# An eighth P buffer, seven output rows on GpSimd and a new table of order in an attention and routed-MLP kernel

## The chip, the cores and the metric

The kernel runs on one core of one Trainium2 chip. The core has TensorE (PE: matrix products into PSUM), ScalarE (ACT: activation functions), VectorE (DVE), GpSimd (POOL) and a queue engine for DMAs (SP). The metric is device microseconds of one execution. Times of several runs are given as their median; an execution taken with the hardware profiler has its own time.

## What is computed

One layer over 2048 tokens of width 448: layer norm, attention with 16 heads of 28 that share one key and one value head, a residual, and then a second layer norm whose rows feed a router; the eight tokens with the highest router score go through a gated MLP, and its weighted result is added to their rows.

```python
x = A_x                                             # [1, 2048, 448]
xn = layernorm(x)
q = xn @ wq                                         # 16 heads of 28
k, v = xn @ wk, xn @ wv                             # one head for all
p = softmax(q k^T * 28 ** -0.5)
h = x + concat_heads(p v) @ wo
n = layernorm(h)
r = n @ w_r
idx = argsort(-r)[:8]
y = (silu(n[idx] @ w_gate) * (n[idx] @ w_up)) @ w_down
out = h + n + scatter(idx, y * sigmoid(r[idx]))
```

## The kernel before

**Blocks and tiles.** The queries are cut into 4 blocks of 512 (qb) and the heads into 4 groups of 4 (g); b = 4 qb + g counts the 16 blocks. The keys are cut into 16 tiles j of 128. One (b, j) is a tile of work. Its scores are two pairs of matmuls (p = 0, 1), each pair 128 keys by 2 heads by 512 queries, which fills two PSUM banks of 512 f32 columns.

**Two ways through the softmax.** A tile goes to ScalarE or to VectorE.

- ScalarE (`act_unit`, L1008): each score pair is one exponential over 128 x 1024 (L1012), from PSUM into a slot of P, a ring of NPB = 6 slots (L309). A pair and the next one use banks 0 and 1 or 2 and 3 in turn, so a score pair must wait until the exponential before the last one is done. `act_pv` (L1015) then multiplies the two slots of a tile by the values: one group of four matmuls side by side (32 x 512 each).
- VectorE (`dve_unit`, L1020): the exponential is made out of the bits of a 16-bit number. Each score pair, in banks 4 and 5, is clamped into 16-bit integers Y (L1024), and three copies shifted by a constant (`shift`, L1028, operation on L1031) are made of the tile; four groups of value matmuls (`dve_pv`, L1036), one per copy with values scaled to fit, average the error out. Y is a ring of 3 tiles. For the tiles that `shared` marks, the third shift is done by GpSimd.

**Around the blocks.** `chunk` (L670) prepares 512 tokens at a time: statistics, normalized rows, transposes, keys and values. `q_project` makes the queries of a block two blocks ahead. `post_block` copies a block's sums (L751), sends the denominators through memory to spread them over the partitions, and scales the result on GpSimd into On (L767). When four groups are done, `out_proj` (L780) makes 128 rows of h: projection on TensorE, residual and statistics on VectorE, the inverse root on GpSimd (L795), and for qb below 2 the output row h + n (L802), a scaling of 128 x 448 f32 on VectorE into outf, which lies over x in SBUF. `out_rows` stores two such rows in one DMA of the SP queue. `first_top`, `first_max` and `second_top` search the highest router scores of the first 1536 tokens inside block 15; the small cast into topb is L856. Behind the last exponential comes a serial tail: the last block's rows, the search, the MLP for eight tokens, and an indirect store from `fin`, which lies in wq_sb.

**What sets the order.** Every operation is recorded with an engine, an assumed duration, what it reads and writes and a priority (`G.op`). `plan` (L113) goes through them as a list scheduler would and fixes the order of the instructions on each engine; the program is emitted in that order, with semaphores where needed. An engine runs its list strictly in order, so what is written behind a waiting instruction waits too. Two rules matter here. For TensorE, score pairs for ScalarE are marked `crit`: another operation is put ahead of one that will soon be ready only if it would make it late by no more than SLACK, and TensorE is left idle for it if that is shorter than WAIT. Operations marked `lock` (all of GpSimd, and VectorE's shifts and some others) are planned so that they don't overlap; a GpSimd operation gets a wait for the last such VectorE operation planned ahead of it, while VectorE gets none for GpSimd.

The priorities come from tables at the top of the file. For each block from 2 on, TILES says which key tiles go to VectorE, how many of them have the third shift on GpSimd, and an offset in time. EARLY lists the VectorE tiles of blocks 0 and 1, QUERY, ROWS and CHUNK place the projections, the output rows and the preparation. Before, the tables hold 58 + 4 = 62 tiles for VectorE, 33 of them shared, and 194 for ScalarE.

Of the kernel before, what the change touches and what calls it, by code (L numbers as in the profile page):

```python
# [16 lines left out]
SLACK, WAIT = 248.0, 240.0  # L17
# [4 lines left out]
    2: ((0, 5, 8, 13), 4, -0.95),  # L22
    3: ((0, 3, 6, 10, 13), 3, 0.94),
    4: ((2, 8, 10, 12), 2, 1.48),
    5: ((1, 4, 6, 11), 0, 1.34),
    6: ((2, 6, 11, 13), 2, -0.37),
    7: ((1, 3, 8, 11, 13), 2, 1.13),
    8: ((4, 9, 11, 13), 0, 1.08),
    9: ((5, 7, 12), 3, 0.03),
    10: ((0, 5, 8, 10, 12), 3, 1.5),  # L30
    11: ((2, 4, 9, 12), 1, -0.68),
    12: ((0, 2, 4, 8), 4, 0.5),
    13: ((0, 2, 6, 9, 11), 5, 0.63),
    14: ((2, 10, 12), 3, 1.18),
    15: ((0, 4, 8, 10), 1, 0.33),
# [3 lines left out]
EARLY = [(0, 5, 18.21), (0, 15, 22.04), (0, 4, 23.54), (1, 12, 28.01)]  # L39
QUERY = {2: 12.3, 3: 12.3, 4: 6.9, 5: 7.0, 6: 11.5, 7: 11.1, 8: 8.7, 9: 10.4, 10: 6.7, 11: 9.5, 12: 10.1, 13: 7.6}  # L40
ROWS = {
    (0, 0): 10.9, (0, 1): 7.3, (0, 2): 10.3, (0, 3): 9.3, (1, 0): 10.7, (1, 1): 11.9, (1, 2): 13.1,
    (1, 3): 9.9, (2, 0): 6.2, (2, 1): 11.4, (2, 2): 8.4, (2, 3): 9.2
}
CHUNK = (0.0, 5.1, 10.9, 36.9)
# [255 lines left out]
def _main(nc, G, sb, ps, psb, flag, scr, xs, ptab, A_x, A_wq, A_wk, A_wv, A_wo, B_w_r, B_w_gate, B_w_up, B_w_down, out,  # L301
# [8 lines left out]
    NPB = 6  # L310
# [12 lines left out]
    idi = sb("idi", [128, 128], I32)  # L323
# [45 lines left out]
    junk = sb("junk", [128, D], BF16)  # L369
    outf = x_sb[:, :, 0:D]  # L370
# [42 lines left out]
    onesb = sb("onesb", [128, 128], BF16)  # L413
    bz = sb("bz", [128, 3, 8], BF16)
    onesh = sb("onesh", [128, 128], F16)
# [4 lines left out]
    eg = sb("eg", [128, NFC, 8], F32)  # L420
    sg = sb("sg", [128, NFC, 8], F32)
# [10 lines left out]
    def pk(b):  # L432
        return ("ps", b)
# [28 lines left out]
    for i in range(4, NT, 4):  # L462
        dma(x_sb[:, i:i + 4, 0:D], x_v[:, i:i + 4, :], [("x", t) for t in range(i, i + 4)], lat=3500.0 + 400 * i,
            reads=[("x", 3)])
    G.op(PO, lambda e: e.iota(idi[:, :], [[1, 128]], base=0, channel_multiplier=-1), 250, writes=["idi"])
    G.op(PO, lambda e: e.tensor_single_scalar(ident[:, :], idi[:, :], 0, ALU.is_equal), 560,
         reads=["idi"], writes=["ident"])
# [40 lines left out]
    def kk(j, p):  # L508
        return ("K0", min(j, 2), p) if j < 4 else ("K", j // 4, p)
# [25 lines left out]
    def late_consts(gate):  # L535
# [16 lines left out]
        G.op(PO, lambda e: e.memset(onesb[:, :], 1.0), 200, writes=["onesb"])  # L552
        G.op(PO, lambda e: e.memset(bz[:, :, :], 0.0), 100, writes=["bz"])
        G.op(PO, lambda e: e.memset(onesh[:, :], 1.0), 200, writes=["onesh"])
# [6 lines left out]
        G.op(PO, lambda e: e.iota(idi[0:8, 0:96], [[1, 96]], base=0, channel_multiplier=0), 250, writes=["idi"])  # L561
# [485 lines left out]
    for m, (b, j, t) in enumerate(dve_tiles):  # L1047
        for p in range(2):
            at(t + 1.5 * p, dve_unit, m, b, j, p, t + 1.5 * p)
        for v in (1, 2, 3):  # L1050
            at(t + 1.6 + 0.5 * v, shift, m, v, b)
# [295 lines left out]
```

## Time and profile before

| | us |
|---|---|
| median of 3 runs (387.9 to 390.82) | 388.7 |
| the profiled execution, its own time | 387.67 |
| its span, first to last instruction | 385.9 |
| busy: ScalarE / TensorE / VectorE / GpSimd | 374.1 / 344.0 / 338.2 / 115.0 |
| first exponential starts | 9.47 |
| ScalarE goes on to the first instruction behind the last exponential | 365.88 |

How to read the rows that follow. A row of a timeline has the start and the length in us from the span's start, the engine, the line of the kernel, the operation, what it writes and reads (buffer numbers left out), shapes, and how many instructions the row merges. A row of a group has the shape, the count, then busy us and the mean ns of one, then the idle time of the engine just before them and what ended it. A row of windows has a stretch and its length, then for each engine the busy time and the number of instructions, then the granted clock, the share of the DMA engines and GB/s. Matmuls overlap and their ends are modelled; starts are what to go by. The granted TensorE clock is 0.984 of full speed over the span.

### The profile page before, as it was taken

To read this page: it belongs to the slowest core of one execution; us is meant where nothing else is said; L and a number is where in the kernel's file an instruction comes from. 1 tells how busy PE (TensorE), PEld (TensorE's weight loads), DVE (VectorE), ACT (ScalarE), POOL (GpSimd) and SP (SyncE) were. 2 spreads that over 40 slices of the span, in tenths; PEclk is the share of its full clock that TensorE was granted. 3 is DMA by queue.
4 is the path that set the end of the run, shared out by engine and by line. 5 is a ranking of instruction groups with operands and counts; after the bars stand their busy time and mean duration, and the time that the engine had idled before them with its cause. 6 is when DMAs were issued, how large, how long until landed. Compare 5 with 4: busy or idle time off the path is not lost.

```text
span 385.9 us, 8129 instructions
## 1 busy us (share of the span) xinstructions
PE 344.0 (89%) x3361; PEld 105.6 (27%) x3361; DVE 338.2 (88%) x613; ACT 374.1 (97%) x433; POOL 115.0 (30%) x149
## 2 busy tenths in 40 slices
PE   7799898989988999899998988999898999888945
PEld 7333222222222222222222222222222222222324
DVE  6985888888998999989999989999999998999382
ACT  6999999999999999999999999999999999999992
POOL 7440002544123112404101244402145454431100
PEclk9999999999999999999999999999999999999985
DMA  8696000100000000201001000011001010100011
GB/s 208 163 235 190 2 2 12 49 2 29 2 27 5 4 29 26 77 1 54 2 14 63 7 27 27 28 50 31 26 30 51 3 53 27 52 26 20 14 51 55
DMA packets 18045, 17.12 MB, mean 44 GB/s; under 512 B 6660, under 2 KB 15124, under 8 KB 18004
## 3 DMA queue, kind: packets, MB, share of 16 engines
q1 hardware_dynamic: 17652, 16.32, 14.7%
q8 instruction: 27, 0.44, 0.5%
q10 hardware_dynamic: 288, 0.23, 0.2%
q14 instruction: 14, 0.11, 0.1%
q0 software_dynamic: 64, 0.02, 0.0%
HBM read 11.70 MB, written 4.86 MB: 43 GB/s over the span
## 4 chain that ended last, share of the span: by engine, by line
ACT 92%; PE 3%; DVE 3%; DMA 1%; issue 0%; SPq 0%; POOL 0%; POOLq 0%
ACT P L1012 90%; PE ps L436 3%; DMA wq_sb<-in_A_wq_dram 1%; ACT xn L964 1%; DVE Y L1024 1%; DVE topb L856 0%; DVE bn L934 0%; SPq L449 0%; ACT x_sb L825 0%; DVE Y L1031 0%; ACT xnT L618 0%; POOL out_dram L1239 0%; ACT Rb L741 0%; ACT Rb L739 0%; ACT wq_pad L491 0%
## 5 line engine op out<-in xcount | busy, mean ns | idle before, releaser
L1012 ACT ACTIVATE P<-ps 128x1024 bf16<-128x1024 f32 x388 | 356.3, 1132 | 1.4 <-PE ps L436 1.3
L436 PE MATMUL ps<-Q,K 64*128 64x512 bf16 x1024 | 179.9, 385 | 29.3 <-ACT P L1012 25.0
L1024 DVE TENSOR_SCALAR Y<-ps 128x1024 int16<-128x1024 f32 x124 | 151.2, 1219 | 19.8 <-PE ps L436 19.5
L1031 DVE TENSOR_SCALAR Y<-Y 128x2048 int16<-128x2048 int16 x153 | 100.4, 685 | 0.5
L436 PEld LDWEIGHTS ps<-Q,K 64*128 64x128 bf16 x1024 | 44.7, 93 | 175.4 <-ACT P L1012 152.7
L1031 POOL TENSOR_SCALAR Y<-Y 128x2048 int16<-128x2048 int16 x33 | 62.6, 1898 | 96.4 <-DVE Y L1031 87.6
L436 PE MATMUL ps<-Y,Vs 128*32 128x512 bf16 x992 | 84.9, 383 | 0.0
L436 PE MATMUL ps<-P,Vs 128*32 128x512 bf16 x776 | 76.3, 388 | 0.1
L767 POOL TENSOR_TENSOR On<-Ot,Rb 128x512 bf16<-128x512 f32 x15 | 19.1, 1273 | 45.5 <-DVE Y L1031 30.6
L436 PEld LDWEIGHTS ps<-Y,Vs 128*32 128x32 bf16 x992 | 23.8, 95 | 27.3 <-issue 17.5
L436 PEld LDWEIGHTS ps<-P,Vs 128*32 128x32 bf16 x776 | 19.6, 93 | 42.5 <-issue 41.7
L763 POOL TENSOR_TENSOR Ls<-Ls,Lc 128x16 f32<-128x16 f32 x15 | 4.2, 280 | 68.2 <-DVE Y L1031 60.9
L436 PE MATMUL ps<-xnT,wq_pad 112*128 112x512 bf16 (+1 forms) x68 | 19.2, 371 | 0.6 <-DVE K L643 0.5
L436 PE MATMUL ps<-wo_pad,On 128*128 128x448 bf16 (+1 forms) x64 | 17.5, 358 | 1.0 <-DVE On L745 1.0
L517 DVE TENSOR_SCALAR Q<-ps,qone 128x512 bf16<-128x512 f32 x15 | 11.0, 734 | 1.7 <-PE ps L436 1.7
L795 POOL TENSOR_TENSOR hbuf<-st,nhalf 128x1 f32<-128x1 f32 x12 | 6.6, 552 | 14.3 <-DVE Y L1031 10.3
L751 DVE COPY Ot<-ps 128x512 f32<-128x512 f32 x15 | 10.3, 684 | 0.7 <-PE ps L436 0.4
L804 DVE SCALAR_TENSOR_TENSOR junk<-hbuf,w_rb 128x448 bf16<-128x448 f32 x12 | 8.1, 677 | 0.0
L789 DVE TENSOR_TENSOR hbuf<-ps,x_sb 128x448 f32<-128x448 f32 x12 | 7.4, 618 | 0.3 <-PE ps L436 0.2
L791 DVE BATCH_NORM_STATS2 bn<-hbuf 128x6 f32<-128x448 f32 x12 | 7.4, 618 | 0.1
L719 DVE TENSOR_SCALAR K<-ps,ksc,kb 128x512 bf16<-128x512 f32 x6 | 4.6, 803 | 3.3 <-PE ps L436 3.3
L1239 POOL DMA_INDIRECT out_dram<-wq_sb,idxc x1 | 0.9, 930 | 20.8 <-DVE wq_sb L1238 20.8
(209 smaller groups left out, 172.1 us busy)
## 6 DMA issues: line engine op xcount, KB each, us to landing
Rb<-h_scr SPq DMA_DIRECT2D x15, 256.0 KB
h_scr<-hbuf SPq DMA_DIRECT2D x12, 225.0 KB, 2.2
out_dram<-x_sb SPq DMA_DIRECT2D x8, 224.0 KB, 2.5
wg_sb<-in_B_w_gate_dram SPq DMA_DIRECT2D x1, 1568.0 KB, 12.2
wu_sb<-in_B_w_up_dram SPq DMA_DIRECT2D x1, 1568.0 KB, 18.7
wd_sb<-in_B_w_down_dram SPq DMA_DIRECT2D x1, 1568.0 KB, 22.1
x_sb<-in_A_x_dram SPq DMA_DIRECT2D x3, 448.0 KB, 5.6
wo_pad<-in_A_wo_dram SPq DMA_DIRECT2D x4, 98.0 KB
```

The lines of the kernel that those rows point to most:

```text
L436: return lambda e: e.matmul(o, lhsT=l, rhs=r, start=start, stop=stop)
L517: G.op(DV, lambda e: e.tensor_scalar(Q[:, b % 4, :], ps[:, bank, :], qone[:, 0:1], None, ALU.add), dvt(512), reads=[pk(bank), "qone"], wri ...
L719: G.op(DV, lambda e, bank=bank, c=c, p=p: e.tensor_scalar(K[:, p, c * 512:(c + 1) * 512], ps[:, bank, :], ksc[:, p:p + 1], kb[:, p:p + 1], ...
L751: G.op(DV, lambda e: e.tensor_copy(Ot[:, rb, :], ps[:, acc_bank(b), :]), dvt(512), reads=[pk(acc_bank(b))], writes=[("Ot", rb)], prio=u - 30)
L767: G.op(PO, lambda e: e.tensor_tensor(On[:, qb % 2, g, :], Ot[:, rb, :], Rb[:, rb, :], ALU.mult), 1270, reads=[("Ot", rb), ("Rb", rb)], wri ...
L789: G.op(DV, lambda e: e.tensor_tensor(h, ps[:, bank, 0:D], x_sb[:, t, 0:D], ALU.add), dvt(D), reads=[pk(bank), ("x", t)], writes=[("h", hr)])
L791: G.op(DV, lambda e: e.bn_stats(bn6[:, t, :], h), dvt(D), reads=[("h", hr)], writes=[("bn6", t)])
L795: G.op(PO, lambda e: e.tensor_tensor(s4, st[:, t, 7:8], nhalf[:, 0:1], ALU.pow), 570, reads=[("st7", t), "nhalf"], writes=[("h4", hr)])
L804: G.op(DV, lambda e: e.scalar_tensor_tensor(junk[:, :], h, s4, w_rb[:, :], ALU.mult, ALU.mult, accum_out=st[:, t, 2:3]), 700, reads=[("h", ...
L1012: marks["exp"] = G.op(AC, lambda e: e.activation(P[:, sl, :, :], ps[:, b0:b0 + 2, :], ACT.Exp, bias=EBIAS, scale=OCT), 905, reads=[pk(b0), ...
L1024: G.op(DV, lambda e: e.tensor_scalar(Y[:, n, 0, p:p + 3:2, :].bitcast(I16), ps[:, 4:6, :], 0.0, 32639.0 - 3 * STEP, ALU.max, ALU.min), 114 ...
L1031: G.op(PO if po else DV, lambda e: e.tensor_scalar(Y[:, n, v, :, :].bitcast(I16), Y[:, n, 0, :, :].bitcast(I16), 1.0, v * STEP, ALU.mult, ...
```

## The change

- **P ring**: NPB goes from 6 to 8 slots. To make room, some small tiles lose their own memory: the index tile `idi` now lies in `junk`, the constant tiles `onesb` and `onesh` and the MLP's `eg` and `sg` lie in `wq_sb`, which is free once its padded copy is made. An iota into `idi` that nothing read is dropped.
- **Output rows**: of the 8 rows t = 0 to 7 that `out_proj` scales, seven (all but 6) are scaled by GpSimd.
- **VectorE's offsets**: the distance in priority of a tile's score pairs, clamps and shifts from its own time was fixed in the code (-2.9, -2, 2.1, 2.6, 3.1 by way of the event's time) and comes from the table PACE now. GpSimd's shift is planned with 1930 ns instead of 2030.
- **Tables**: all are new, SLACK and WAIT among them. They hold 60 + 4 = 64 tiles for VectorE, 45 of them shared, and 192 for ScalarE. Block 4 (in which `last_w` does its reductions on VectorE) has three VectorE tiles and none shared; blocks 9 and 12 have five tiles, all shared.

```diff
-SLACK, WAIT = 248.0, 240.0
+SLACK, WAIT = 144.0, 159.0
 TILES = {
-    2: ((0, 5, 8, 13), 4, -0.95),
+    2: ((0, 2, 6, 12), 4, -1.5),
...
 }
-CHUNK = (0.0, 5.1, 10.9, 36.9)
+POOLROWS = [0, 1, 2, 3, 4, 5, 7]
+PACE = (-6.4, -1.8, 1.1, -3.6, 1.5, 2.8)
+CHUNK = (0.0, 6.3, 7.4, 13.5)
...
-    NPB = 6
+    NPB = 8
...
-    idi = sb("idi", [128, 128], I32)
+    idi = junk[:, 0:256].bitcast(I32)
...
-    onesb = sb("onesb", [128, 128], BF16)
+    onesb = wq_sb[:, 1, 0:128]
...
-    onesh = sb("onesh", [128, 128], F16)
+    onesh = wq_sb[:, 2, 0:128].bitcast(F16)
...
-    eg = sb("eg", [128, NFC, 8], F32)
-    sg = sb("sg", [128, NFC, 8], F32)
+    eg, sg = (wq_sb[:, 3, 224 * k:224 * k + 224].bitcast(F32).rearrange("p (c n) -> p c n", n=8) for k in range(2))
...
         if qb < 2:
-            G.op(DV, lambda e: e.tensor_scalar(outf[:, t, :], h, st[:, t, 5:6], s6, ALU.mult, ALU.add), 420,
-                 reads=[("h", hr), ("st5", t), ("h6", hr)], writes=[("outf", t)], lock=True)
+            on = t in POOLROWS
+            G.op(PO if on else DV, lambda e: e.tensor_scalar(outf[:, t, :], h, st[:, t, 5:6], s6, ALU.mult, ALU.add),
+                 900 if on else 420, reads=[("h", hr), ("st5", t), ("h6", hr)], writes=[("outf", t)], lock=True)
...
-        G.op(PE, qk(4, b, j, p), 216, reads=[("Q", b % 4), ("Qh", b % 4), kk(j, p)], writes=[pk(4), pk(5)], prio=t - 2.9,
-             form=1)
+        G.op(PE, qk(4, b, j, p), 216, reads=[("Q", b % 4), ("Qh", b % 4), kk(j, p)], writes=[pk(4), pk(5)],
+             prio=t + PACE[0] + (PACE[2] - 1.5) * p, form=1)
         G.op(DV, lambda e: e.tensor_scalar(Y[:, n, 0, p:p + 3:2, :].bitcast(I16), ps[:, 4:6, :], 0.0,
                                            32639.0 - 3 * STEP, ALU.max, ALU.min), 1140, reads=[pk(4), pk(5)],
-             writes=[("Y", n, 0, p)], prio=t - 2)
+             writes=[("Y", n, 0, p)], prio=t + PACE[1] + (PACE[2] - 1.5) * p)
...
-                                                         1.0, v * STEP, ALU.mult, ALU.add), 2030 if po else 605,
+                                                         1.0, v * STEP, ALU.mult, ALU.add), 1930 if po else 605,
...
-             writes=[("Y", n, v)], lock=True)
+             writes=[("Y", n, v)], lock=True, prio=t + PACE[2 + v])
```

How this moves the instructions, at three places. In the rows, a line number is that of the file the row is from (L1031 before is L1032 after); `Q,K` are scores, `x2` being one pair, `P,Vs` and `Y,Vs` are groups of value products, `x4` being one group. Score pairs for ScalarE and for VectorE read alike.

TensorE before, in the middle of the program, the place that the prediction's timeline shows:

```order
L436 MATMUL ps<-Q,K 128x512 x2
L436 MATMUL ps<-P,Vs 32x512 x4
L436 MATMUL ps<-Q,K 128x512 x4
L436 MATMUL ps<-Y,Vs 32x512 x8
L436 MATMUL ps<-P,Vs 32x512 x4
L436 MATMUL ps<-Q,K 128x512 x2
```

TensorE after, some ten score pairs later in the new order:

```order
L437 MATMUL ps<-Q,K 128x512 x2
L437 MATMUL ps<-Y,Vs 32x512 x8
L437 MATMUL ps<-Q,K 128x512 x4
L437 MATMUL ps<-P,Vs 32x512 x4
L437 MATMUL ps<-Q,K 128x512 x2
L437 MATMUL ps<-Y,Vs 32x512 x8
L437 MATMUL ps<-Q,K 128x512 x2
```

Where three groups stood between two score pairs, two stand now, and the next group follows behind a further pair.

GpSimd before, where the rows of the first query block are finished (the power into hbuf is L795, the product into On L767, the sums Ls and Lsi L763 and L761):

```order
L795 TENSOR_TENSOR hbuf<-st,nhalf 128x1
L1031 TENSOR_SCALAR Y<-Y 128x2048
L763 TENSOR_TENSOR Ls<-Ls,Lc 128x16
L761 TENSOR_TENSOR Lsi<-Lsi,Li 128x16
L1031 TENSOR_SCALAR Y<-Y 128x2048
L795 TENSOR_TENSOR hbuf<-st,nhalf 128x1
L767 TENSOR_TENSOR On<-Ot,Rb 128x512
```

GpSimd after, at the second and third of these rows:

```order
L795 TENSOR_TENSOR hbuf<-st,nhalf 128x1
L1032 TENSOR_SCALAR Y<-Y 128x2048
L803 TENSOR_SCALAR x_sb<-hbuf,st 128x448
L1032 TENSOR_SCALAR Y<-Y 128x2048
L763 TENSOR_TENSOR Ls<-Ls,Lc 128x16
L761 TENSOR_TENSOR Lsi<-Lsi,Li 128x16
L1032 TENSOR_SCALAR Y<-Y 128x2048
L795 TENSOR_TENSOR hbuf<-st,nhalf 128x1
L767 TENSOR_TENSOR On<-Ot,Rb 128x512
L803 TENSOR_SCALAR x_sb<-hbuf,st 128x448
```

A scaled row (L803, new on this engine) follows each power, and the shifts stand closer together.

VectorE before, in block 15, around the search for the highest router scores:

```order
L1031 TENSOR_SCALAR Y<-Y 128x2048
L853 MAX top<-v_row 1x8
L1031 TENSOR_SCALAR Y<-Y 128x2048
L854 MAX_INDEX idx<-top,v_row 1x8
L856 CAST topb<-top 1x8
L1024 TENSOR_SCALAR Y<-ps 128x2x512
```

VectorE after, from the shift that GpSimd's last shift waits for (the first row) to the same cast:

```order
L1032 TENSOR_SCALAR Y<-Y 128x2048
L1025 TENSOR_SCALAR Y<-ps 128x2x512
L844 MAX top<-ps 12x8
L845 MAX_INDEX idx<-top,ps 12x8
L1025 TENSOR_SCALAR Y<-ps 128x2x512
L847 TENSOR_SCALAR pos<-idx,p 12x8
L1032 TENSOR_SCALAR Y<-Y 128x2048
L854 MAX top<-v_row 1x8
L755 RECIPROCAL Li<-Lc 128x16
L855 MAX_INDEX idx<-top,v_row 1x8
L857 CAST topb<-top 1x8
```

Before, GpSimd's last shift waited for the second L1031 of the rows shown, one row ahead of the search behind which the cast stands; now it waits for a shift ten rows ahead of the cast.

51 lines of the change are left out of this document (25 added, 26 removed).

## Prediction, made before the changed kernel ran

> **What bounds the kernel now.** I read the page's totals and its chain first, then the chain in order of time, then ScalarE's own timeline, and last TensorE's timeline at one late exponential. Totals and chain (the second line gives the chain's shares of the span by line):
>
> ```profile
> PE 344.0 (89%) x3361; PEld 105.6 (27%) x3361; DVE 338.2 (88%) x613; ACT 374.1 (97%) x433; POOL 115.0 (30%) x149
> ...
> ACT P L1012 90%; PE ps L436 3%; DMA wq_sb<-in_A_wq_dram 1%; ACT xn L964 1%; DVE Y L1024 1%; DVE topb L856 0%; DVE bn L934 0%; SPq L449 0%; ACT x_sb L825 0%; DVE Y L1031 0%; ACT xnT L618 0%; POOL out_dram L1239 0%; ACT Rb L741 0%; ACT Rb L739 0%; ACT wq_pad L491 0%
> ```
>
> ScalarE's exponentials (L1012) are nine tenths of the chain; three engines are near 90% busy, so it can change hands. The chain in time (start, us, what):
>
> ```profile
> 9.47 59.75 ACT P L1012 x65
> ...
> 344.61 1.76 DVE topb L856
> 346.37 1.13 DVE Y L1024
> ...
> 347.55 1.71 PE ps L436 x18
> ...
> 349.28 16.61 ACT P L1012 x18
> 365.88 1.25 ACT x_sb L825 x2
> ```
>
> The exponentials run from 9.47 to 365.88: 356.41 us. The head of 9.5 us and the tail of 385.9 - 365.88 = 20.0 us stand around them. The same engine's timeline, for a stretch in which nothing comes late (start, us busy, instructions):
>
> ```profile
> 53.52 11.12 ACT L1012 ACTIVATE P<-ps 128x1024 bf16<-128x1024 f32 x12
> 64.37 1.18 ACT L1012 ACTIVATE P<-ps 128x1024 bf16<-128x1024 f32 x1
> ```
>
> Twelve starts in 64.37 - 53.52 = 10.85 us: 0.904 us each. The mean duration of 1132 ns in the groups below is longer because consecutive ones overlap, so an exponential may start up to 0.2 us late and the page still shows no idle time. At 0.904 the 388 would take 350.8 us; they take 356.4, so **5.7 us of lateness** is in the stage, of which the page calls only 1.4 idle. One late place, TensorE's timeline:
>
> ```profile
> 137.28 0.39 PE L436 MATMUL ps<-Q,K 64*128 64x512 bf16 x2
> 137.60 0.40 PE L436 MATMUL ps<-P,Vs 128*32 128x512 bf16 x4
> 137.93 0.60 PE L436 MATMUL ps<-Q,K 64*128 64x512 bf16 x4
> 138.47 0.61 PE L436 MATMUL ps<-Y,Vs 128*32 128x512 bf16 x8
> 138.91 0.39 PE L436 MATMUL ps<-P,Vs 128*32 128x512 bf16 x4
> 139.23 0.39 PE L436 MATMUL ps<-Q,K 64*128 64x512 bf16 x2
> ```
>
> And ScalarE's (the first row ends with the exponential that the second shows alone):
>
> ```profile
> 138.66 2.17 ACT L1012 ACTIVATE P<-ps 128x1024 bf16<-128x1024 f32 x2
> 139.66 1.17 ACT L1012 ACTIVATE P<-ps 128x1024 bf16<-128x1024 f32 x1
> ```
>
> Three groups of P and Y products stand between two score pairs (Q,K) for ScalarE. From 137.93 two pairs take 0.54 to the next start, Y x8 takes 0.44, P 0.32: so a pair or a group is 0.22 us and a change between the two kinds 0.1. Pair to pair this gap costs 0.22 + 3 x 0.22 + 2 x 0.1 = 1.08 us, above 0.904, and the exponential that starts at 139.66 comes 1.00 after the one at 138.66, 0.1 late.
>
> **The change, part by part.** The rows by shape that carry the prices (busy us, mean ns):
>
> ```profile
> L1012 ACT ACTIVATE P<-ps 128x1024 bf16<-128x1024 f32 x388 | 356.3, 1132 | 1.4 <-PE ps L436 1.3
> L1024 DVE TENSOR_SCALAR Y<-ps 128x1024 int16<-128x1024 f32 x124 | 151.2, 1219 | 19.8 <-PE ps L436 19.5
> L1031 DVE TENSOR_SCALAR Y<-Y 128x2048 int16<-128x2048 int16 x153 | 100.4, 685 | 0.5
> L1031 POOL TENSOR_SCALAR Y<-Y 128x2048 int16<-128x2048 int16 x33 | 62.6, 1898 | 96.4 <-DVE Y L1031 87.6 <-DVE junk L902 5.6 <-DVE st L793 1.7
> L767 POOL TENSOR_TENSOR On<-Ot,Rb 128x512 bf16<-128x512 f32 x15 | 19.1, 1273 | 45.5 <-DVE Y L1031 30.6 <-DMA Rb<-h_scr 10.1 <-DVE x_sb L807 2.9
> L802 DVE TENSOR_SCALAR x_sb<-hbuf,st 128x448 bf16<-128x448 f32 x8 | 4.1, 508 | 0.0
> L699 POOL TENSOR_SCALAR xn<-x_sb,nmean,rstd 128x448 bf16<-128x448 bf16 x5 | 3.5, 713 | 1.1 <-DVE xn L695 0.8
> ```
>
> 1. *Tiles.* The tables hold 62 tiles for VectorE before and 64 now, so ScalarE has 194 x 2 = 388 exponentials before and 192 x 2 = 384 now. Four fewer on the chain: 4 x 0.904 = **-3.6 us**, as long as ScalarE stays the chain.
>
> 2. *VectorE* gets 4 clamps (151.2 / 124 = 1.22 each, +4.9). Its shifts fall from 153 to 147, because 45 instead of 33 of the 192 go to GpSimd (100.4 / 153 = 0.66 each, -3.9), and 7 of its 8 output rows leave (0.51 each, -3.6). Sum -2.6 of 338.2 in a span some 5 shorter: its share stays 88%. I cost this at nothing; the cover is the 20.1 us idle that the rows of L1024 and L1031 show, and a clamp that comes late would hold TensorE, in order, ahead of the next pair for ScalarE.
>
> 3. *TensorE's order.* I priced the work between consecutive pairs for ScalarE in both orders by the 0.22 and 0.1 above. Over 1.0 us are 99 of 387 gaps before and 48 of 383 now, although the mean gap rises from 0.79 to 0.82 us (two more Y tiles, more changes of kind). Without the place in point 4, 5.7 - 0.5 = 5.1 us of lateness lie on 99 long gaps, 0.052 us each; 48 of them make 2.5: **-2.6 us**. The ends are 0 (the lateness only moves) and -5.1 (all goes); I take the share by count, since the row at 139.66 shows the mechanism. The eighth buffer has no price of its own: ScalarE's row shows no wait for a free one that could be told from a wait for scores. It lets the P groups be put later, which the count holds already.
>
> 4. *The cast of topb* near the end. VectorE there, and one row of GpSimd:
>
> ```profile
> 344.54 1.83 DVE L856 CAST topb<-top 1x8 bf16<-1x8 f32 x1
> 347.42 0.15 DVE L857 CAST posf<-idx 1x8 f32<-1x8 uint32 x1
> 344.45 1.90 POOL L1031 TENSOR_SCALAR Y<-Y 128x2048 int16<-128x2048 int16 x1 [3.11 <-DVE Y L1031]
> ```
>
> ScalarE's next exponentials:
>
> ```profile
> 346.93 1.19 ACT L1012 ACTIVATE P<-ps 128x1024 bf16<-128x1024 f32 x1
> 348.19 1.02 ACT L1012 ACTIVATE P<-ps 128x1024 bf16<-128x1024 f32 x1
> ```
>
> A cast of eight numbers took 1.83 us, until GpSimd's shift ended, where the next cast took 0.15. The chain above runs from that cast over the clamp behind it and TensorE to the exponential at 349.28. The starts 346.93, 348.19, 349.28 are 1.26 and 1.09 apart, together 0.54 us more than 2 x 0.904. In the new order GpSimd's last shift waits only for a VectorE shift that stands ahead of two clamps and both searches, (the clamps alone take over 2 us), so its 1.90 us are over before the cast: **-0.5 us**, between 0 and that. Late next there could be the search of v_row, which now follows the first search after one clamp and one shift and needs a copy through memory to have landed.
>
> 5. *GpSimd.* 12 more shifts (1.90 each, +22.8) and 7 rows. No row shows a 448-wide f32 row scaled there: from below 0.71 (L699, the same two operands in bf16), from above 1.273 x 448 / 512 = 1.11 (L767, two f32 tensors). I take 0.9, between the two, +6.3: 115 becomes 144 us. The work hides behind the exponentials unless VectorE and GpSimd meet. Behind a late shift stands a Y group on TensorE and behind that the scores; behind a late row the SP queue's store of two rows, and behind that the sums' round trip through memory that On waits for. Whole stage, then the densest stretch (VectorE and GpSimd; two rows with all instructions, then the same two with the shifts alone):
>
> ```profile
> 9.47:365.88 356.41, 326.33 (x3033) 91.41 (x3031) 320.99 (x533) 356.27 (x389) 106.97 (x116) 1.00 0.14 40
> 299.39:319.47 20.08, 19.54 (x184) 5.17 (x178) 19.46 (x34) 20.08 (x24) 9.79 (x8) 1.00 0.08 27
> 9.47:365.88 356.41, 100.39 (x153) 62.62 (x33) 1.00 0.14 40
> 299.39:319.47 20.08, 6.62 (x10) 7.59 (x4) 1.00 0.08 27
> ```
>
> The third and fifth engine figures of the first two rows are VectorE and GpSimd. If a VectorE shift and any GpSimd work exclude each other, the pair was taken for 106.97 + 100.39 = 207 of 356 us in the stage and 9.79 + 6.62 = 16.4 of 20.1 in that stretch. It will be taken for about 207.4 + 22.8 + 6.3 - 3.9 = 232.6 of 351, and in blocks 9 and 12 (five tiles, all five third shifts on GpSimd, one row) nearly all the time: 5 x 1.90 + 1.27 + 0.9 for GpSimd and 10 x 0.66 for VectorE are 18.3, which leaves 1.6 of the block's 22 x 0.904 = 19.9 for the small operations of both. So some new waits are to be expected. The one such meeting priced above cost 0.54. The bounds are 0 and, with one meeting for each of the 19 moved instructions, 19 x 0.54 = 10.3; I take three, **+1.6 us**, near the lower end, because 33 shifts have shown one.
>
> 6. *The rest.* The ids in junk and the ones and the gate's tiles in wq_sb add no instruction, and one iota of GpSimd goes; the chain's shares by line name GpSimd only for the last store. In the new order TensorE's and ScalarE's rows up to the first exponential and behind the last stand as they were. No term.
>
> Sum: -3.6 - 2.6 - 0.5 + 1.6 = -5.1. The profiled execution (387.67, span 385.9) would come to 382.6; the median of the runs shown is 388.7, 1.0 above it, and there the same sum gives **383.6 us**.
>
> **Rivals.** *The lateness stays* (B): the gaps get fewer but the mean gap grows, and late Y groups put back what the shorter gaps give. For it speaks TensorE's 19.54 of 20.08 in the row above; against it, that the long gaps halve. Only the four exponentials count: 388.7 - 3.6 = 385.1. *Nearly all lateness goes* (D): 388.7 - 3.6 - 5.1 - 0.5 = 379.5; against it, the 48 gaps that remain. *The meetings decide* (C), the slower side: GpSimd's third shift comes late, TensorE stands at its Y group, and ScalarE's scores wait behind. At 0.54 each it takes (3.6 + 2.6 + 0.5) / 0.54, some 12 meetings, to eat the gain; with 19 the time is 388.7 - 6.7 + 10.3 = 392.3. For it: the cast, and blocks 9 and 12. Against it: in the densest stretch now, the 22 exponentials from 299.3 to 319.45 are 0.25 us late in all.
>
> [...]
>
> **How the numbers follow.** My forecast (A) 0.52, its own range 381.5 to 384.8; B 0.26; C 0.12; D 0.10. The time is A's. The range goes from 380.5, which leaves out the better half of D, to 386.8, which takes in B with another 1.7 us, three meetings more, and leaves out C. A change of 1%, 3.9 us, is about what a measurement of this kernel can tell from none: below 384.8 lie A and D (0.62), within it B (0.26), above it C (0.12).
>
> **What would show it.** ScalarE's group reads x384 and its stage from the first exponential to the next L826 some 351 us, 3 to 5 us over 384 x 0.904 = 347.1. Near the end no cast of topb lasts 1.8 us. GpSimd is busy some 144 us, VectorE's share stays near 88%. I am wrong if the chain of waits hands more than a few per cent to VectorE's shifts or GpSimd, if shifts on VectorE of over 0.75 us become many, or if the late exponentials follow clamps and not groups of products.

## The result, and the profile of the changed kernel

The changed kernel takes 384.75 us (median of 4 runs, 384.36 to 385.57), the kernel before 388.64 beside it (4 runs, 387.9 to 390.82): a ratio of 0.991, 95% interval 0.989 to 0.993. The number is inside the range on record and 1.2 us above the forecast. Its working was wrong in two terms of opposite sign, -2.6 and +1.6, as will be seen, so that it came this close is in part luck.

The profiled execution took 385.57 us, with a span of 383.8. From the page, the totals, the granted clock in 40 slices, and the chain by engine and by line:

```profile
PE 355.4 (93%) x3385; PEld 105.7 (28%) x3385; DVE 340.5 (89%) x604; ACT 370.8 (97%) x429; POOL 142.4 (37%) x167
...
PEclk9999999999998999999999999999999999998965
...
ACT 91%; PE 6%; DVE 2%; POOL 0%; issue 0%; POOLq 0%
ACT P L1013 90%; PE ps L437 5%; DVE bn L935 0%; ACT x_sb L826 0%; DVE Y L1025 0%; POOL out_dram L1240 0%; PE ps L440 0%; ACT Rb L741 0%; DVE idx L1144 0%; DVE Ot L751 0%; DVE top L1143 0%; ACT Rb L739 0%; DVE Y L1032 0%; POOL ident L467 0%; DVE On L745 0%
```

ScalarE still carries the chain; VectorE has 2% of it and GpSimd less than 1%. The clock row has an 8 in the 13th and in the 37th slice, where the kernel before has 9s up to its tail; that is new. The groups by shape:

```profile
L1013 ACT ACTIVATE P<-ps 128x1024 bf16<-128x1024 f32 x384 | 352.8, 1186 | 2.1 <-PE ps L437 2.0
L1025 DVE TENSOR_SCALAR Y<-ps 128x1024 int16<-128x1024 f32 x128 | 155.8, 1217 | 17.9 <-PE ps L437 16.2
L1032 POOL TENSOR_SCALAR Y<-Y 128x2048 int16<-128x2048 int16 x45 | 85.5, 1901 | 102.7 <-DVE Y L1032 102.7
L1032 DVE TENSOR_SCALAR Y<-Y 128x2048 int16<-128x2048 int16 x147 | 100.7, 709 | 0.7
...
L803 POOL TENSOR_SCALAR x_sb<-hbuf,st 128x448 bf16<-128x448 f32 x7 | 5.0, 719 | 15.5 <-DVE Y L1032 12.3
```

The exponentials are 384 and start at 10.00; the first and the last on ScalarE's timeline, and the cast of topb on VectorE's:

```profile
10.00 1.02 ACT L1013 ACTIVATE P<-ps 128x1024 bf16<-128x1024 f32 x1 [1.17 <-PE ps L437]
...
362.50 1.17 ACT L1013 ACTIVATE P<-ps 128x1024 bf16<-128x1024 f32 x1
363.41 0.88 ACT L826 ACTIVATE x_sb<-hbuf,st 128x448 bf16<-128x448 f32 x1
```

```profile
347.37 0.14 DVE L857 CAST topb<-top 1x8 bf16<-1x8 f32 x1
```

From the first start to the last end (362.50 + 1.17) the stage takes 353.7 us (353.4 to the start of the L826 that the prediction's test names), not the 351 that the test asked for. By the prediction's price it would be 6.5 us over 384 x 0.904 = 347.1, more lateness than before (5.7), although the long gaps are halved as counted. So the price had to be looked at again, and the kernel's own rows before the change held the answer. ScalarE's timeline of the kernel before, around the exponential at 139.66 that the prediction called 0.1 us late, one instruction a row:

```profile
136.85 1.23 ACT L1012 ACTIVATE P<-ps 128x1024 bf16<-128x1024 f32 x1
137.76 1.24 ACT L1012 ACTIVATE P<-ps 128x1024 bf16<-128x1024 f32 x1
138.66 1.25 ACT L1012 ACTIVATE P<-ps 128x1024 bf16<-128x1024 f32 x1
...
140.58 1.17 ACT L1012 ACTIVATE P<-ps 128x1024 bf16<-128x1024 f32 x1
```

Add start and length. The ends are 138.08, 139.00, 139.91, then 140.83 for the one quoted in the prediction (139.66 + 1.17), then 141.75: all 0.92 apart. The late start cost nothing. Starts are recorded 0.904 apart, and each instruction is recorded 0.0125 longer than the one before it; what a late start takes away is that overlap. The changed kernel shows the edge of it:

```profile
85.89 1.34 ACT L1013 ACTIVATE P<-ps 128x1024 bf16<-128x1024 f32 x1
87.08 1.07 ACT L1013 ACTIVATE P<-ps 128x1024 bf16<-128x1024 f32 x1
88.15 1.02 ACT L1013 ACTIVATE P<-ps 128x1024 bf16<-128x1024 f32 x1
```

The start at 87.08 is 0.28 late and its end, 88.15, is 0.92 after 87.23: free. The next one is 0.17 late, is down at 1.02 (as long as the first one, at 10.00, which follows a wait of 1.17), and its end, 89.17, is 1.02 after: 0.1 lost.

The theory of the experiments, called the period theory in the expectations: ScalarE completes one exponential each 0.9166 us, a late start is paid out of an overlap of up to 0.32 us (1.34 - 1.02), and time is lost only where that is used up. "Lost" below is the sum over all exponentials of how far an end lies more than 0.9166 behind the end before it (differences under 0.005 left out), worked out from the records of starts and lengths. The stage is then the first one's extra 0.11 (1.02 - 0.917), count x 0.9166, and what is lost:

| | count | stage | count x 0.9166 | lost |
|---|---|---|---|---|
| before | 388 | 356.4 | 355.6 | 0.65 |
| changed, profile above | 384 | 353.7 | 352.0 | 1.59 |
| changed, third profile (e11) | 384 | 352.5 | 352.0 | 0.36 |

Before, 0.34 of the 0.65 is lost at the two exponentials behind the cast of topb, and only 0.3 elsewhere, in TensorE's order. In the changed kernel 0.35 is lost at three places of TensorE's order (at 25.8, 89.2 and 217.9 us); in the profile above 1.2 more goes at 121.6 and from 346 to 349, where the clock row has its 8s. The rivals are the prediction's own theory (0.904 and 0.052 us for each long gap, the "gap theory") and its third rival, the meetings of VectorE and GpSimd.

### The profile page after: what moved, and what is told of

Its sections match the earlier page's. It is cut to its first block, busy times and chain, and to the rows that moved or that the text cites. A ratio compares the mean times of both kernels' runs of the same rounds, so it can differ in the third digit from the quotient of the medians.

```text
span 383.8 us, 8193 instructions
## 1 busy us (share of the span) xinstructions
PE 355.4 (93%) x3385; PEld 105.7 (28%) x3385; DVE 340.5 (89%) x604; ACT 370.8 (97%) x429; POOL 142.4 (37%) x167
## 3 DMA queue, kind: packets, MB, share of 16 engines
HBM read 11.70 MB, written 4.86 MB: 43 GB/s over the span
## 4 chain that ended last, share of the span: by engine, by line
ACT 91%; PE 6%; DVE 2%; POOL 0%; issue 0%; POOLq 0%
ACT P L1013 90%; PE ps L437 5%; DVE bn L935 0%; ACT x_sb L826 0%; DVE Y L1025 0%; POOL out_dram L1240 0%; PE ps L440 0%; ACT Rb L741 0%; DVE idx L1144 0%; DVE Ot L751 0%; DVE top L1143 0%; ACT Rb L739 0%; DVE Y L1032 0%; POOL ident L467 0%; DVE On L745 0%
## 5 line engine op out<-in xcount | busy, mean ns | idle before, releaser
L1013 ACT ACTIVATE P<-ps 128x1024 bf16<-128x1024 f32 x384 | 352.8, 1186 | 2.1 <-PE ps L437 2.0
L1025 DVE TENSOR_SCALAR Y<-ps 128x1024 int16<-128x1024 f32 x128 | 155.8, 1217 | 17.9 <-PE ps L437 16.2
L1032 POOL TENSOR_SCALAR Y<-Y 128x2048 int16<-128x2048 int16 x45 | 85.5, 1901 | 102.7 <-DVE Y L1032 102.7
L1032 DVE TENSOR_SCALAR Y<-Y 128x2048 int16<-128x2048 int16 x147 | 100.7, 709 | 0.7
L437 PE MATMUL ps<-Y,Vs 128*32 128x512 bf16 x1024 | 90.9, 385 | 0.0
L437 PEld LDWEIGHTS ps<-Y,Vs 128*32 128x32 bf16 x1024 | 22.6, 94 | 35.6 <-issue 32.6
L767 POOL TENSOR_TENSOR On<-Ot,Rb 128x512 bf16<-128x512 f32 x15 | 19.1, 1274 | 23.2 <-DVE Y L1032 10.7
L795 POOL TENSOR_TENSOR hbuf<-st,nhalf 128x1 f32<-128x1 f32 x12 | 6.6, 553 | 25.7 <-DVE Y L1032 18.6
L763 POOL TENSOR_TENSOR Ls<-Ls,Lc 128x16 f32<-128x16 f32 x15 | 3.3, 223 | 20.2 <-DVE junk L895 11.7
L803 POOL TENSOR_SCALAR x_sb<-hbuf,st 128x448 bf16<-128x448 f32 x7 | 5.0, 719 | 15.5 <-DVE Y L1032 12.3
```

What stands on the lines that cost most here:

```text
L437: return lambda e: e.matmul(o, lhsT=l, rhs=r, start=start, stop=stop)
L767: G.op(PO, lambda e: e.tensor_tensor(On[:, qb % 2, g, :], Ot[:, rb, :], Rb[:, rb, :], ALU.mult), 1270, reads=[("Ot", rb), ("Rb", rb)], wri ...
L795: G.op(PO, lambda e: e.tensor_tensor(s4, st[:, t, 7:8], nhalf[:, 0:1], ALU.pow), 570, reads=[("st7", t), "nhalf"], writes=[("h4", hr)])
L803: G.op(PO if on else DV, lambda e: e.tensor_scalar(outf[:, t, :], h, st[:, t, 5:6], s6, ALU.mult, ALU.add), 900 if on else 420, reads=[("h ...
L1013: marks["exp"] = G.op(AC, lambda e: e.activation(P[:, sl, :, :], ps[:, b0:b0 + 2, :], ACT.Exp, bias=EBIAS, scale=OCT), 905, reads=[pk(b0), ...
L1025: G.op(DV, lambda e: e.tensor_scalar(Y[:, n, 0, p:p + 3:2, :].bitcast(I16), ps[:, 4:6, :], 0.0, 32639.0 - 3 * STEP, ALU.max, ALU.min), 114 ...
```

## Experiments

**The changed kernel once more (e1), and its clock.** Nothing is edited.

> The changed kernel once more, nothing edited. In its first profile the granted clock fell to one half for two windows of 3.413 us (118.79 and 344.07), each behind a window in which TensorE was busy about 0.6 of the time; ends of exponentials lost 0.31 us in the first and 0.92 in the second. Period theory (ScalarE ends one exponential each 0.917 us, 384 of them make 352.0 of the stage's 353.7 us, and the halved clock explains most of the rest): the windows lie otherwise from run to run, so one profile may show none, one or two halved windows, and the span follows: about 382.5 with none, up to 383.8 with two; median of the times within 0.3% of 384.75. Rival (the light stretches have nothing to do with it): halved windows at other places than behind these two stretches, and a span that does not go with them.

Measured: 385.51 us (6 runs, 384.01 to 387.71), ratio 0.993 [0.991, 0.996]; in the profile one halved window, at 343.7, and 1.45 us lost. Windows of 3.413 us of the first profile of the changed kernel (columns as in the prediction: TensorE's busy us come first, the granted clock stands before the DMA share):

```profile
115.38:118.79 3.41, 1.96 (x17) 0.50 (x14) 3.41 (x11) 3.41 (x5) 0.00 (x0) 1.00 0.15 52
118.79:122.20 3.41, 3.34 (x20) 0.57 (x16) 3.41 (x5) 3.21 (x4) 1.27 (x1) 0.50 0.06 25
340.65:344.07 3.42, 2.07 (x13) 0.58 (x13) 3.03 (x6) 3.42 (x5) 0.97 (x1) 1.00 0.19 70
344.07:347.48 3.41, 3.28 (x20) 0.69 (x22) 3.20 (x12) 2.92 (x4) 1.28 (x3) 0.50 0.03 3
```

And of the second:

```profile
115.03:118.44 3.41, 2.14 (x16) 0.51 (x16) 3.41 (x10) 3.41 (x5) 0.00 (x0) 1.00 0.10 32
340.31:343.72 3.41, 2.08 (x13) 0.58 (x13) 3.02 (x7) 3.41 (x5) 0.86 (x1) 1.00 0.19 70
343.72:347.13 3.41, 3.17 (x20) 0.70 (x22) 3.15 (x11) 2.92 (x4) 1.23 (x2) 0.50 0.03 3
```

The three windows here in which TensorE was busy for 1.96 to 2.08 of 3.41 us were each followed by one at half clock (a dip, below); the windows lie elsewhere in each run, and with 2.14 us in the first stretch nothing followed. The first stretch is block 4, which has three tiles for VectorE now and no GpSimd work; the second is where TensorE has little but score pairs and waits for VectorE's router scores ahead of the first search. That a light stretch lies ahead of each dip is shown; the next run takes the light stretches away.

**Idle products in the light stretches (e2).** Behind pairs 114 to 124 and 360 to 364, in the order as planned (FILL gives for a pair how many products, and the free bank that they write; they are 21, not the 20 of the expectation):

```diff
+FILL = {114: (2, 7), 115: (1, 7), 116: (2, 7), 117: (1, 7), 118: (2, 7), 120: (2, 7), 121: (1, 7), 122: (1, 7), 124: (2, 7), 360: (1, 7), 361: (1, 7), 362: (1, 7), 363: (2, 6), 364: (2, 6)}
...
+                self.orders[PE].insert(self.orders[PE].index(p) + 1, o)
...
+    G.idle_mm = lambda bank: mm(ps[:, bank, :], K[0:64, 0, 0:128], Q[0:64, 0, :], True, True)
```

> The changed kernel with 20 idle products of 512 columns put behind score pairs for ScalarE in the two stretches where TensorE is lightly busy (pairs 114 to 124 and 360 to 364), the order otherwise as it is. If a lightly busy window is what halves the clock: no halved window at either place in any run, mean clock 0.982 to 0.984 in all, the 1.2 us that ends of exponentials lost there gone, profiled span 382.3 to 382.8, median 0.3 to 1.2 us below the changed kernel's on the same chip. Rival, the halving has another cause or is hidden: the dips stay, or go without the time moving; time within 0.3 of the changed kernel's. Rival, the products themselves make the pairs behind them late: 0.2 us for each, some 2 us slower.

Measured: 386.3 us (385.36 to 386.54), ratio 0.994 [0.993, 0.996]. Both dips are gone (clock 0.982), and the time is not lower: 1.91 us are lost, 1.22 of it at one exponential at 358.9. The expected gain did not come, because another wait came up. From the chain, GpSimd's and TensorE's timelines of this run:

```profile
347.02 3.35 DMA h_scr<-Li
350.37 0.02 issue
350.39 5.16 DMA Rb<-h_scr
...
355.63 1.27 POOL On L786
```

```profile
356.95 0.56 PE L456 MATMUL ps<-wo_pad,On 128*128 128x450 bf16 x2 [1.26 <-POOL On L786]
```

The denominators of block 14 go through memory before On can be made, and TensorE stands 1.26 us at the first early product for the last rows, with score pairs behind it. It is tempting to say that the dip had hidden this wait, since in the first profile On is done at 356.37, 0.7 ahead of that product at 357.05. But the unedited kernel without a dip (e11, below) has no wait either:

```profile
h_scr<-Li SPq DMA_DIRECT2D x1, 8.0 KB, 1.4
```

```profile
354.70 1.27 POOL L767 TENSOR_TENSOR On<-Ot,Rb 128x512 bf16<-128x512 f32 x1
```

```profile
356.30 0.56 PE L437 MATMUL ps<-wo_pad,On 128*128 128x450 bf16 x2
```

What differs is the write of the denominators (Li): 1.4 us in all six profiles of the changed order without the idle products, 2.9 to 3.4 us in the three with them (e2, e8, e12). In those three, the queue that loads instructions (q8) has a transfer of 16 KB under way before the write has landed, in e2 from 347.87 to 349.40; in the other six it comes after that (at 351.19 in the first profile). So it comes earlier in the runs with the 21 added instructions. DMA rows of e2 from 347.0 to 350.4:

```profile
q8 instruction: 1, 0.02, 2.8%
...
h_scr<-Li SPq DMA_DIRECT2D x1, 8.0 KB, 3.4
```

So the idle products took one wait away, and another came with them. That it is the transfer that delays the write is inferred: no run moves it alone.

**GpSimd's third shifts cut short (e3).**

```diff
+        c = slice(0, 16 if po else 512)
-        G.op(PO if po else DV, lambda e: e.tensor_scalar(Y[:, n, v, :, :].bitcast(I16), Y[:, n, 0, :, :].bitcast(I16),
+        G.op(PO if po else DV, lambda e: e.tensor_scalar(Y[:, n, v, :, c].bitcast(I16), Y[:, n, 0, :, c].bitcast(I16),
```

> The changed kernel with GpSimd's 45 third shifts cut to 16 of 512 columns each (most of the third copy is left out; order and waits as they are). GpSimd's busy time falls from 142 to about 65 us and its shifts block VectorE no longer. Period theory: ScalarE's ends lost nothing to these meetings, so the time stays within 0.4 us of the changed kernel's on the same chip. Meetings theory (the prediction's term of +1.6 us, 0 to 10.3): 1.6 us faster or more; by the ten VectorE shifts above 700 ns in the profile, some 4 us of VectorE, at most 4 us faster.

Measured: 385.64 us, ratio 0.993 [0.991, 0.995], against 385.51 for the changed kernel on the same chip. Groups of this run:

```profile
L1033 POOL TENSOR_SCALAR Y<-Y 128x64 int16<-128x64 int16 x45 | 11.0, 244 | 131.8 <-DVE Y L1033 131.8
```

```profile
L1033 DVE TENSOR_SCALAR Y<-Y 128x2048 int16<-128x2048 int16 x147 | 97.2, 686 | 0.7
```

The meetings are real: without them VectorE's shifts take 686 ns on average and not 709, 3.5 us in all. ScalarE gets nothing of it: the medians differ by 0.1 us where the meetings theory asked for 1.6 or more, and the ends lose 1.34 us, 0.34 of it at the three places of TensorE's order as in the first profile and 0.98 behind a halved window at 344.9. The meetings theory falls.

**Long gaps cut in the kernel before (e4).** Of 80 groups of value products in gaps over 0.9 us one small matmul is left:

```diff
+            for o in lst[a:b]:
+                if work() > 900.0 and o.cut and not o.done:
+                    o.fns, o.done = [o.cut], True
```

> The kernel before, with 80 groups of value products (four matmuls of 512 columns) cut to one matmul of 16 columns, so that of TensorE's 99 gaps over 1.0 us between score pairs for ScalarE 17 are left (the cut groups' part of the sums is left out; order and waits as they are). Gap theory, as the prediction had it (an exponential each 0.904 us and 0.052 us of lateness for each long gap): 82 x 0.052 = 4.3 us faster, 384.3. Period theory (one each 0.917 us, a late start is taken out of an overlap of up to 0.32 us and costs nothing unless that is used up): the ends show 0.65 us lost in the whole stage, 0.34 of it at the cast of topb and not touched, so 0.1 to 0.3 us faster, 388.3 to 388.6.

Measured: 388.04 us (11 runs), ratio 0.9989 [0.998, 0.9998]: 0.5 us faster, not 4.3. The group and the first and last exponential of this run:

```profile
L1030 ACT ACTIVATE P<-ps 128x1024 bf16<-128x1024 f32 x388 | 355.8, 1240 | 1.1 <-PE ps L454 1.1
```

```profile
10.68 1.02 ACT L1030 ACTIVATE P<-ps 128x1024 bf16<-128x1024 f32 x1 [1.08 <-PE ps L454]
...
365.28 1.18 ACT L1030 ACTIVATE P<-ps 128x1024 bf16<-128x1024 f32 x1
```

From the first end, 11.70, to the last, 366.46, are 354.76 us for 387: 0.9167 each, and 0.01 lost. This is the floor for 388 exponentials, and the kernel before is 0.6 us above it. The gap theory falls.

One part of the expectation missed: the 0.34 us behind the cast of topb was to stay. The cast is as long as before and the exponential behind it starts as late, but nothing is lost there:

```profile
345.28 1.83 DVE L874 CAST topb<-top 1x8 bf16<-1x8 f32 x1
```

```profile
347.69 1.34 ACT L1030 ACTIVATE P<-ps 128x1024 bf16<-128x1024 f32 x1
...
348.94 1.02 ACT L1030 ACTIVATE P<-ps 128x1024 bf16<-128x1024 f32 x1
```

The exponential ahead of the late one is 1.34 us long here, against 1.19 for the same one before (the row at 346.93 in the prediction): the overlap is full, and it covers a start 0.33 late. So the cast cost time only where TensorE's order had used the overlap up, and the two can't be priced apart.

**The eighth buffer alone (e5).** Before's tables, rows and offsets in the changed code:

```diff
-POOLROWS = [0, 1, 2, 3, 4, 5, 7]
-PACE = (-6.4, -1.8, 1.1, -3.6, 1.5, 2.8)
+POOLROWS = []
+PACE = (-2.9, -2.0, 1.5, 2.1, 2.6, 3.1)
```

> The kernel before with the ring of P of eight slots instead of six, the small tiles moved into junk and wq_sb, and nothing else: its own tables, rows on VectorE, and the order of every engine as before, so that only the waits for a free slot come later. Period theory (an exponential each 0.917 us, nothing waits for a slot): no change, ratio 0.998 to 1.002, 0.3 to 0.7 us lost in the ends. Rival (slots are waited for, and the eighth buffer itself is the gain): 1 to 3 us faster.

Measured: 388.74 us (10 runs), ratio 1.0002 [0.9988, 1.0016]; 0.65 us lost, at the same exponentials as before. Nothing waited for a slot.

**Eight exponentials left out (e6).** A slice cuts what these exponentials read and write:

```diff
+LEFT = tuple(range(130, 354, 28))
...
+        c = slice(0, 4 if n in LEFT else 512)
```

> The changed kernel with eight of the 384 exponentials, one each 28 from the 131st on, cut to 4 of 512 columns (most of their part of P is left out); order, waits and TensorE's work as they are. Period theory: each goes for 0.917 us less what the small one takes (some 0.2), so about 8 x 0.72 = 5.7 us faster than the changed kernel on the same chip, 379.5 to 380.3. Rival, TensorE, 93% busy, is the bound as much as ScalarE: the pairs behind each cut come no earlier, and 0 to 2 us go. Prediction's price (0.904): 5.6, not to be told from the first.

Measured: 382.69 us (4 runs), ratio 0.984 [0.981, 0.987]: 2.2 to 2.8 us less than the changed kernel (e11 on the same chip later, e1 on another), half of what the period theory expected and more than its rival did. TensorE and ScalarE behind the first cut (the small one ends at 130.13; the eight are recorded with 339 ns on average, where some 0.2 us was estimated):

```profile
130.11 0.39 PE L438 MATMUL ps<-Q,K 64*128 64x512 bf16 x2 [0.28 <-ACT P L1015]
```

```profile
130.54 1.02 ACT L1015 ACTIVATE P<-ps 128x1024 bf16<-128x1024 f32 x1 [0.42 <-PE ps L438]
```

The next pair had to wait until the exponential two before (end 130.06) freed its two banks, so the next one starts 0.49 and ends 1.51 behind that end, in place of 1.83: 0.32 saved at each cut, 2.6 in all. One exponential alone is not worth 0.917; only one that goes with its pair, as in the tables, can be. This run doesn't price the exponential; e4 and the table above do.

**The early products without the wait (e7), and both together (e8).** The half that reads only blocks 12 and 13 no longer waits for block 14:

```diff
+            if p == 0:
+                o.drop = G.last_w["On", 1, 2][0].idx
```

> The changed kernel, order as it is, in which the first half of the last rows' early products (heads of blocks 12 and 13) no longer waits for the On of block 14, which only the second half reads. In the run with idle products the denominators of block 14 came back late (3.35 us for the write of Li in place of 1.4) and TensorE stood 1.26 us at the first half, with 1.22 us lost in ScalarE's ends. If that round trip is what spreads the times of the changed kernel (384.0 to 387.7): the spread narrows to 1.5 us or less, no loss in the ends near 358, median 0.3 to 1.5 us below the changed kernel's 385.5 on this chip's like; with the halved clock still there at 344. Rival, the spread has another source: times as the changed kernel's, 384 to 387.7.

Measured: 385.64 us (384.72 to 386.82), ratio 0.992 [0.990, 0.995]. No gain: the dip at 344.7 is still there, 1.37 us are lost, 0.96 of it at the dip, and the write of Li takes 1.4 us, so there was no wait to save. The round trip does not explain the spread.

> Both together: the idle products in the two light stretches and the first half of the early products without the wait for block 14. If the halved clock near 344 and the round trip each hide the other (without the dip the products come to the wait about 1 us earlier): neither alone gains much, both together lose 0.3 to 0.6 us in the ends of the stage, span 382 to 383, median 383.5 to 384.6, 1 us or more below the changed kernel on the same chip. Rival: as the run with idle products alone, 385.4 to 386.5.

Measured: 384.57 us (384.25 to 384.98), ratio 0.990 [0.988, 0.992], 0.38 us lost and none of it at a dip or at the round trip. The write of Li takes 2.9 us here too, and the second edit keeps TensorE from waiting for it. The idle products alone come with the late write, the second edit alone has nothing to take away; both together take 1.1 us off e7 on the same chip.

**The new tables with six slots (e9).** The order is planned anew:

```diff
-    NPB = 8
+    NPB = 6
```

> The changed kernel with the ring of P back at six slots and everything else as changed, the tables too; the planner then orders anew, since P groups must be done earlier to free slots. TensorE's gaps over 1.0 us are 78 then in place of 48. Gap theory: 30 x 0.052 = 1.6 us slower than the changed kernel, 386.4 to 387. Period theory: worked through pair by pair (a pair starts when TensorE is free and the exponential two before has ended, an exponential ends 0.917 after the last one or 1.02 after its start, whichever is later) this order loses 3.4 us in the ends by TensorE's work alone and 6.9 with VectorE's waits in the plan, where the changed order by the same working loses 0.4 to 0.9: 3 to 6 us slower, 388 to 391. Rival: the eighth buffer matters as little in the new tables as alone, within 0.5 us of 385.

Measured: 389.16 us (10 runs), ratio 1.0008 [0.9992, 1.0025]. All of the gain is gone. 5.15 us are lost, at 35 exponentials, between the 3.4 and the 6.9 that were worked out pair by pair; 0.5 of it stands behind a halved window at 120.1. The group:

```profile
L1013 ACT ACTIVATE P<-ps 128x1024 bf16<-128x1024 f32 x384 | 354.9, 1113 | 3.4 <-PE ps L437 2.4
```

The mean of 1113 ns beside 1186 in the changed kernel says the same: the overlap is used up often.

**The new tables with the rows on VectorE (e10).** The order is planned anew:

```diff
-POOLROWS = [0, 1, 2, 3, 4, 5, 7]
+POOLROWS = []
```

> The changed kernel with the seven output rows back on VectorE and everything else as changed; the planner orders anew. Gaps over 1.0 us: 62. Gap theory: 14 x 0.052 = 0.7 us slower than the changed kernel, about 386. Period theory, worked as for the run with six slots: 2.1 us lost in the ends by TensorE's work alone, 5.3 with VectorE's waits, against 0.4 to 0.9: 1.7 to 4.4 us slower, 387 to 390. Rival (VectorE has 18 us idle and takes seven rows of 0.51 without notice): within 0.5 us of 385.

Measured: 388.8 us (10 runs), ratio 1.0001 [0.998, 1.002]. Again all of the gain is gone: 3.43 us are lost in the stage, 1.8 more than in the changed kernel's first profile; 0.97 of it behind two halved windows at 117.3. Another 2.3 come from the tail, 22.4 us behind the last exponential (387.4 - 365.0) where it was 20.1. Most of this is TensorE, which comes late to the last value products, and VectorE waits for their sums. First the changed kernel, then e10:

```profile
363.46 0.66 PE L437 MATMUL ps<-P,Vs 128*32 128x512 bf16 x8
```

```profile
366.60 0.60 PE L437 MATMUL ps<-P,Vs 128*32 128x512 bf16 x8
```

```profile
367.27 0.44 DVE L735 STREAM_SHUFFLE Ot<-ps 128x256 f32<-128x256 f32 x1
```

The last exponential ends at 363.68 in the one and 365.01 in the other, so these products start 0.2 us ahead of that end in the changed kernel and 1.6 behind it here.

**Both kernels side by side (e11, e12).** The last two are the changed kernel unedited and the version of e8 on one chip.

> The changed kernel unedited, beside the next run on one chip. By the accounting of the ends (384 x 0.9166 = 352.0, the first one's 0.1, 0.4 lost in TensorE's order, 0.5 to 1.2 lost in halved clocks or at the round trip of block 14): median 384.4 to 385.6, with a spread of 1.5 us or more.

> The changed kernel with idle products in the two light stretches and without the wait for block 14 in the first half of the early products, as in the earlier run, now beside the changed kernel on one chip. If the 0.38 us lost in the ends there was no luck: again 0.3 to 0.6 us lost, median 384.2 to 384.9, 0.4 to 1.2 us below the changed kernel's, spread under 1 us. Rival (the two kernels don't differ by more than the chips do): medians within 0.3 us.

Measured: 384.86 us (384.67 to 386.09), ratio 0.990 [0.988, 0.993], and 384.18 us (383.86 to 384.82), ratio 0.988 [0.985, 0.990]. The profile of e11 had no dip; its light windows held a little more, 2.16 and 2.22 us:

```profile
116.55:119.96 3.41, 2.16 (x20) 0.53 (x18) 3.41 (x10) 3.41 (x5) 0.00 (x0) 1.00 0.19 74
341.82:345.23 3.41, 2.22 (x19) 0.70 (x19) 3.38 (x8) 3.41 (x6) 1.90 (x1) 1.00 0.01 2
```

It lost 0.36 us, e12 0.51. The version with both fixes is 0.7 us below on this chip; the intervals overlap. Over all chips its 10 runs lie from 383.86 to 384.98, the changed kernel's 15 unedited ones from 384.01 to 387.71. It is the fastest version found that leaves nothing out, and what it does is take the upper runs away.

A further part of the spread lies ahead of the stage. The first exponential starts between 9.47 and 10.68 us in the fourteen profiles, whatever the kernel: at 9.47 before, at 10.37 in e5, whose order is the same, at 10.00, 9.84 and 10.47 in the three of the changed kernel. It is the later the later the trace first records the full clock (at 4.79 us before, 6.15 in the first profile of the changed kernel, 7.76 in e4). Why that moment moves no run here tests. So the profile of e4 is 1.1 us longer than that of before although its stage is 0.6 shorter, and spans are to be compared stage by stage.

## Why the prediction's number was right, and two of its terms wrong

1. *Tiles, -3.6.* Right. 4 x 0.9166 = 3.7, and it is nearly the whole gain: the medians are 3.9 us apart, the stages of the profiles 2.7 to 3.9 (356.4 before, 352.5 to 353.7 after). The price was read from starts, which are 0.904 apart; ends are what count.
2. *VectorE, nothing.* Right in cost, wrong in size: 340.5 us busy where 2.6 less than 338.2 were worked out. Its shifts got longer (709 ns on average, 685 before), and e3 shows that this costs ScalarE nothing.
3. *TensorE's order, -2.6.* This step failed. The 5.7 us of lateness that the prediction saw did not exist: 0.65 us was lost, 0.3 of it at TensorE's order alone. The long gaps did halve, and e4 took 82 of 99 away from the kernel before for 0.5 us, all that there was to gain; the changed order loses 0.35 at three places, as much as before. The bound was wrong as well: "ends 0 and -5.1" held the right value only at its edge, and it was set aside because an exponential 0.1 late was seen without looking at its end. The page had the contrary evidence: the group's busy time, 356.3 us, was the stage.
4. *The cast of topb, -0.5.* Right in place: it takes 0.14 us now. Measured by ends it was worth 0.34, and that not by itself: in e4 it lasts 1.83 us and costs nothing.
5. *GpSimd, +1.6.* Right in work (142.4 us busy where 144 were predicted, a row 0.72 where 0.9 was taken), wrong in cost. There were more meetings: ten shifts of VectorE are over 0.75 us, three before, which is one of the signs of being wrong that the prediction named. VectorE paid 3.5 us for them, but e3 shows that none reached ScalarE, so the sign was badly chosen. The row that the price of 0.54 was taken from was a small cast with a score clamp behind it and the overlap gone; a late shift with overlap in hand need not be that (e4 shows even the cast cost nothing with the overlap full).
6. *The rest, nothing.* The clock was missed: halved windows are worth 0 to 1.2 us by where they fall, and the prediction had no term for them. The round trip of block 14 costs nothing in the changed kernel's own three profiles.

The two wrong terms are -2.6 and +1.6; what is left of them, -1.0, is nearly the whole distance of the forecast from the time. Without them the sum is -3.6 - 0.5, which gives 384.6 for a median of 388.7: the measured time, and the neighbourhood of the rival "the lateness stays" (385.1), which had a chance of 0.26. The forecast's own range, 381.5 to 384.8, held the time by a hair. Of its tests, the count, the cast, GpSimd's and VectorE's share held; the one that failed, a stage of 351 us, was the one that tested step 3. The rival of the meetings needed 12 that cost 0.54 each, and there were none; the one in which nearly all lateness goes had nothing to remove.

One reading of the change has to be corrected too. The prediction gave the eighth buffer no price and the rows none on the path. Alone the buffer does nothing (e5), but without it, or without the rows on GpSimd, these tables gain nothing (e9, e10): they are what lets TensorE and VectorE take two more tiles without using up ScalarE's overlap, and for the rows, about half of what they are worth here lies in the tail. For each, the planner made another order, so what was measured is these tables without the part; tables searched for six slots may do better. The times of the unedited kernel spread by 1.2 to 3.7 us in a session. The halved windows (0 to 1.2 us) and the start of the first exponential (1.2 us over all profiles) are parts of that; the rest is not settled.

## What to carry to other kernels

Where instructions of one engine overlap in the records, take the period from ends, or from busy time over count, before calling a late start lost time (here 0.917 us by ends, 0.904 by starts); a group whose busy time is its stage gains little but by fewer instructions (before, 356.3 of 356.4 us; e4, with 0.01 us lost, had a stage 0.6 us shorter). A part that does nothing alone may be what another part stands on, so take it out of the whole as well. A fix that gains nothing may have brought a wait of its own, as the idle products did here: look at what its own run loses, and whether the unedited kernel ever had that wait. The losses behind one overlap did not add up here (the late start behind the cast of topb lost 0.34 us before and nothing in e4), so price one late start with the others in place.

## What the runs showed of the hardware

- ScalarE's exponentials over 128 x 1024 were recorded to start each 0.904 us until one is 1.34 us long, then each 0.917; ends came each 0.917 throughout (e4: 387 in 354.76). Why starts run ahead no run here shows. The first exponential, which starts behind a wait, was recorded with 1.02 us (the row at 10.00 in the changed kernel, at 10.68 in e4).
- The clock halved for 3.413 us behind windows in which TensorE was busy for 1.96 to 2.10 us (eight of them in seven profiles, at full clock and inside the stage). Windows at full clock with 2.13 us and more were not followed by it; two lower ones, 2.03 in e7 and 2.05 in e4, were not either, so busy time by the records does not settle alone where the clock halved.
- The write of Li, 8 KB, took 1.4 us in the changed kernel near 347 and 3.35 in e2. Of the 210 such writes in the fourteen profiles 58 took over 1.6 us, and in 55 of these a 16 KB transfer of the queue of instructions was under way before the write had landed; ten of the 152 shorter ones had one too.
